# Relu² attention into a gated MLP on one core: 32 more score tiles of the first batch are read back transposed, VectorE rounds some high parts, the first phases are placed anew, and first pairs' own blocks are computed at 128 columns

## The chip, the cores and the metric

The kernel runs on one core of one Trainium2 chip. The metric is device time in microseconds (us). Before the change three runs gave a median of 2008.58 us (2007.91 to 2011.16). The profiled execution, from which all rows below come, took 2007.14 us, of which the traced span is 2005.4 us.

## The reference, cut to what matters

```
scores = (1/S) * z @ z.T                    # 4 batches, S = 3008, z has 64 columns
attn   = maximum(scores, 0) ** 2
x      = u * (attn @ v)                     # v, u: 256 columns
xn     = x / sqrt(mean(x*x) + 1e-6) * rms_g
out    = (silu(xn @ w_gate) * (xn @ w_val)) @ w_out     # 1536 hidden columns
```

The score matrix of a batch is z times its own transpose, so it is symmetric, and so is `attn`.

## The kernel before, in words

**Tiling.** The 3008 tokens of a batch are six query chunks of 512 (the last has 448), taken two at a time: a *pair* `p` is two chunks `k = 0, 1`, numbered `c0` and `c0 + 1`, and a batch has three pairs (`NP = 3`), twelve in all. The keys are 24 tiles `kt` of 128. Phase A of a pair runs 24 *steps*, one per key tile in the order that `order(p)` gives, and each step treats both chunks.

**One step.** For each chunk TensorE makes a 128x512 block of scores in PSUM by two matmuls (L537 with the high part of z, L538 with the low part). ScalarE takes the relu (L549). The square is either VectorE's product of relu and PSUM (L557), or, where the string `SQUARED` has a 1, two ScalarE squares (L580 and L588). Every operand of a later matmul is split into a rounded high part `H` and a low part `L`: ScalarE casts the high part (L582, or the square at L580 gives it), VectorE subtracts (L594). Then six matmuls accumulate attn times v (L674, L675 and L679, twice each). In program order a step `i` emits the scores of step `i + 2` (`emit_s`), the split of step `i + 1` (`emit_l`), the jobs hung on the step, and the value matmuls of step `i` (`emit_av`).

**Kept tiles.** A block computed for query chunk `c` and a key tile of a later chunk `kc` can serve, transposed, as the block of query chunk `kc` and the key tiles of chunk `c`. `keep_tile` makes a copy in 2-byte halves (VectorE L648 or ScalarE L650, as the string `COPIES` says), SyncE's queue stores it to HBM (L654, L656), and `load_turned` reads two key tiles at once by a transposing DMA (L492) into one of six `T` buffers; the block then needs no score matmuls, no relu and no square. In batches 1 to 3 all such blocks are kept; in batch 0 only those that the set `KEPT` lists. A chunk's *own* block (its queries against its own keys) is symmetric in itself: for all chunks but the first of a batch and those of pair 0, the last two of its four key tiles are computed at 256 columns only, and the other half comes transposed from the first two (`keep_half`, `load_half`).

**Phases.** The program runs phase A of pairs 0, 1 and 2 (batch 0) first, then alternates: phase M (the MLP) of pair 0, phase A of pair 3, M of pair 1, A of pair 4, and so on. Beside the first three phases A the kernel prepares the MLP's weights: they are loaded, decoded by five VectorE operations per piece (L216 to L235), added and combined by GpSimd or VectorE (`pool_pieces`, L179 and L183), cast by ScalarE (L297) and stored to HBM (L305). At which of the 72 steps of these phases each of these jobs, each load and each read-back is emitted is read in turn from the table `PLAN` by `place`. Each engine runs its instructions in program order, and SyncE's queue issues its DMAs in program order.

Of the kernel before, what the change touches and what calls it, by code (L numbers as in the profile page):

```python
# [19 lines left out]
P = 128  # L20
CH = 512
# [21 lines left out]
]  # L43
SQUARED = [
    ["000010001101001011110110", "011011110101111001111101"],
    ["010010111011111101100110", "011001011110010110100101"],
    ["100111011011001110101010", "111111110111111101010101"],
]
RESIDENT = [
    ["000000000100000011001000", "000100100000001101001001"],  # L50
    ["101010101000000101000010", "100001000011011010000101"],
    ["101000110101000101101010", "000010001101001000000010"],
]
KEPT = {(4, 5)}
# [11 lines left out]
def kernel(  # L66
# [80 lines left out]
    def hook(phase, slot):  # L147
        if phase[0] == "D":
# [308 lines left out]
    LEADS = (7, 1, 4, 5, 0), (7, 1, 3, 6, 0), (7, 1, 4, 5, 0)  # L457

    def order(p):
        b, c0 = where(p)[:2]  # L460
        if p == 0:
            return list(range(NK))
        first = list(range(4 * (c0 + 1), min(4 * (c0 + 2), NK)))
        last = list(range(4 * c0, 4 * c0 + 4))
        rest = [k for k in range(NK) if k not in first and k not in last]
        turns = [k for k in rest if k < 4 * c0]
        keeps_ = [k for k in rest if k >= 4 * c0]
        of = dict(F=first, L=last, T=turns, K=keeps_)
        return [of[x].pop(0) for x in PATTERNS[c0 // 2]]

    def is_half(p, i, k):

        c, kt = where(p)[1] + k, order(p)[i]
        return p > 0 and c > 0 and kt // 4 == c and kt % 4 >= 2
# [6 lines left out]
    def is_turned(p, i, k):  # L481
        b, c0 = where(p)[:2]
        kc = order(p)[i] // 4
        return kc < c0 + k and keeps(b, kc, c0 + k)

    def load_turned(p, i, k):
        b, c0 = where(p)[:2]
        kt, c = order(p)[i], c0 + k
# [17 lines left out]
    def is_square(p, i, k):  # L506

        return p < LAG and SQUARED[p][k][i] == "1" and not is_turned(p, i, k) and not is_half(p, i, k) and i < NK - 2

    def in_psum(p, i, k):  # L510

        b, c0 = where(p)[:2]
        if p >= LAG or RESIDENT[p][k][i] != "1":
            return False
        c, kt = c0 + k, order(p)[i]
# [8 lines left out]
    def s_product(p, i):  # L524
        b, c0 = where(p)[:2]
        kt = order(p)[i]
        for k in range(2):
            if is_turned(p, i, k):
# [6 lines left out]
            cols = slice(HALF if is_half(p, i, k) else 0, n)  # L535
# [32 lines left out]
    copies = [0]  # L568

    def emit_l(p, i, ks=(0, 1)):  # L570
        b, c0 = where(p)[:2]
        kt = order(p)[i]
        made_ = {}
        highs = {}
        for k in ks:
            n = width(c0 + k)
            a = made_[k] = att[p, i, k]
            hi = highs[k] = moving.tile([P, CH], F32R, tag="H", name="H", bufs=5)
            if is_square(p, i, k):
# [9 lines left out]
        for k in ks:  # L589
            n = width(c0 + k)  # L590
            a, hi = made_[k], highs[k]
            if kt < NK - 1:
# [7 lines left out]
        for k, a in made_.items():  # L600
            c = c0 + k
            n = width(c)
            kc = kt // 4
            if kc == c and c and p > 0 and kt % 4 < 2:
# [3 lines left out]
                def keep_half(a=a, c=c, m=n - HALF):  # L608
# [31 lines left out]
    def keep_tile(b, c, kt, c0, a):  # L640
# [3 lines left out]
        halves = copy_tile(LAG if b or c0 else 0, ("out", "out", "out", "u"))  # L644
# [8 lines left out]
        if b == 0:  # L653
# [753 lines left out]
```

## Time and profile before

| what | value |
|---|---|
| median of three runs | 2008.58 us |
| the profiled execution | 2007.14 us, its span 2005.4 us |
| phases A of pairs 0, 1, 2 | 5.06 to 94, to 180, to 256.95 us |
| phase M of pair 0; phase A of pair 3 | to 346.76; to 431.03 us |
| TensorE busy | 1998.6 us, 8976 matmuls |
| VectorE, ScalarE busy | 1595.5, 1417.0 us |
| GpSimd busy | 166.2 us |
| DMA | 328.37 MB in 355822 packets |

The page gives busy time per engine; the stages above are cut where TensorE's first score matmul of a phase A, or the first MLP matmul of a phase M, starts. Matmuls overlap in the trace, so the time that one takes is read from the starts of successive matmuls and not from its recorded duration. The same holds in part for VectorE and ScalarE, whose successive instructions overlap by about 0.1 us.

### The profile page before, as it was taken

To read this page: it belongs to the slowest core of one execution; us is meant where nothing else is said; L and a number is where in the kernel's file an instruction comes from. 1 tells how busy PE (TensorE), PEld (TensorE's weight loads), DVE (VectorE), ACT (ScalarE), POOL (GpSimd) and SP (SyncE) were. 2 spreads that over 40 slices of the span, in tenths; PEclk is the share of its full clock that TensorE was granted. 3 is DMA by queue.
4 is the path that set the end of the run, shared out by engine and by line. 5 is a ranking of instruction groups with operands and counts; after the bars stand their busy time and mean duration, and the time that the engine had idled before them with its cause. 6 is when DMAs were issued, how large, how long until landed. Compare 5 with 4: busy or idle time off the path is not lost.

```text
span 2005.4 us, 27191 instructions
## 1 busy us (share of the span) xinstructions
PE 1998.6 (100%) x8976; PEld 1672.8 (83%) x8976; DVE 1595.5 (80%) x2712; ACT 1417.0 (71%) x2593; POOL 166.2 (8%) x308
## 2 busy tenths in 40 slices
PE   9999999999999999999999999999999999999999
PEld 7888888888888888888888888888888888888889
DVE  8899888988867877887886786788778687677776
ACT  8898877875766666697575665779658566567565
POOL 0254306000000002100000000310000000000000
PEclk9999999999999999999999999999999999999999
DMA  4245574473484696247347469624644846844343
GB/s 155 78 136 165 132 254 135 150 240 120 122 220 155 162 217 233 90 147 232 136 126 200 168 151 242 211 98 153 225 133 125 214 153 162 205 152 153 123 162 115
DMA packets 355822, 328.37 MB, mean 164 GB/s; under 512 B 222944, under 2 KB 272480, under 8 KB 355680
## 3 DMA queue, kind: packets, MB, share of 16 engines
q1 hardware_dynamic: 355680, 326.64, 54.0%
q8 instruction: 70, 1.15, 0.2%
q14 instruction: 72, 0.59, 0.1%
HBM read 189.73 MB, written 85.72 MB: 137 GB/s over the span
## 4 chain that ended last, share of the span: by engine, by line
PE 99%; ACT 1%; DVE 0%; DMA 0%; issue 0%; SPq 0%; ACTq 0%; DVEq 0%
PE po L674 13%; PE po L675 13%; PE po L679 12%; PE ps L904 11%; PE ps L905 11%; PE ps L906 11%; PE py L932 6%; PE py L933 6%; PE py L936 6%; PE ps L538 4%; PE ps L537 4%; DMA raw<-in_zT 0%; ACT r L549 0%; ACT H L580 0%; PE ps L784 0%
## 5 line engine op out<-in xcount | busy, mean ns | idle before, releaser
L674 PE MATMUL po<-H,vh 128*128 128x512 f32 (+1 forms) x1152 | 446.2, 387 | 0.8 <-ACT H L580 0.8
L675 PE MATMUL po<-H,vl 128*128 128x512 f32 (+1 forms) x1152 | 445.5, 387 | 0.0
L911 ACT COPY s<-ps 128x512 f32<-128x512 f32 (+1 forms) x432 | 249.7, 578 | 208.6 <-PE ps L906 208.3
L904 PE MATMUL ps<-xh,wu 128*128 128x512 f32 (+1 forms) x1008 | 389.7, 387 | 0.0
L905 PE MATMUL ps<-xh,wu 128*128 128x512 f32 (+1 forms) x1008 | 388.4, 385 | 0.0
L906 PE MATMUL ps<-xl,wu 128*128 128x512 f32 (+1 forms) x1008 | 388.3, 385 | 0.0
L679 PE MATMUL po<-L,vh 128*128 128x512 f32 (+1 forms) x1104 | 336.0, 386 | 0.1
L916 ACT CAST hH<-s 128x512 fp32r<-128x512 f32 (+1 forms) x288 | 176.6, 613 | 195.9 <-DVE s L1001 187.6
L921 DVE TENSOR_TENSOR hL<-s,hH 128x512 fp32r<-128x512 f32 (+1 forms) x288 | 198.9, 691 | 96.7 <-ACT hH L916 85.3
L549 ACT ACTIVATE r<-ps 128x512 f32<-128x512 f32 x354 | 195.7, 594 | 97.7 <-PE ps L538 81.2
L674 PEld LDWEIGHTS po<-H,vh 128*128 128x128 f32 x1152 | 216.4, 188 | 43.1 <-ACT H L580 1.6
L675 PEld LDWEIGHTS po<-H,vl 128*128 128x128 f32 x1152 | 216.8, 188 | 39.8
L679 PEld LDWEIGHTS po<-L,vh 128*128 128x128 f32 x1104 | 207.2, 188 | 40.2 <-DVE L L594 1.0
L557 DVE TENSOR_TENSOR r<-ps,r 128x512 f32<-128x512 f32 (+1 forms) x265 | 173.8, 683 | 71.0 <-ACT r L549 70.3
L932 PE MATMUL py<-hH,woh 128*128 128x512 f32 (+1 forms) x576 | 222.1, 386 | 0.3 <-ACT hH L916 0.3
L933 PE MATMUL py<-hH,wol 128*128 128x512 f32 (+1 forms) x576 | 221.8, 385 | 0.0
L904 PEld LDWEIGHTS ps<-xh,wu 128*128 128x128 f32 x1008 | 189.3, 188 | 37.7 <-ACT s L911 2.2
L906 PEld LDWEIGHTS ps<-xl,wu 128*128 128x128 f32 x1008 | 189.3, 188 | 36.1
L905 PEld LDWEIGHTS ps<-xh,wu 128*128 128x128 f32 x1008 | 189.4, 188 | 36.0 <-DMA wu<-wc 0.7
L594 DVE TENSOR_TENSOR L<-r,H 128x512 fp32r<-128x512 f32 (+1 forms) x301 | 200.1, 693 | 9.7 <-ACT r L588 9.4
L936 PE MATMUL py<-hL,woh 128*128 128x512 f32 (+1 forms) x576 | 174.9, 385 | 0.0
L995 DVE TENSOR_TENSOR s<-s 128x512 f32<-128x512 f32 (+1 forms) x144 | 98.0, 680 | 80.3 <-ACT s L911 79.9
(107 smaller groups left out, 2935.0 us busy)
## 6 DMA issues: line engine op xcount, KB each, us to landing
wu<-wc SPq DMA_DIRECT2D x288, 448.0 KB, 4.0
kept<-halves SPq DMA_DIRECT2D x168, 256.0 KB, 2.1
raw<-in_v SPq DMA_DIRECT2D x44, 256.0 KB, 4.1
out_T<-y SPq DMA_DIRECT2D x44, 256.0 KB, 2.0
raw<-in_zT SPq DMA_DIRECT2D x38, 256.0 KB, 4.3
u<-in_uT SPq DMA_DIRECT2D x36, 256.0 KB, 4.0
ux<-xg SPq DMA_DIRECT2D x14, 512.0 KB, 4.2
wc<-wohi SPq DMA_DIRECT2D x21, 256.0 KB, 2.9
```

The lines of the kernel that those rows point to most:

```text
L594: nc.vector.tensor_tensor(lo[:, :n], a[:, :n], f32(hi[:, :n]), op=ALU.subtract)
L674: nc.tensor.matmul(po[d][:, :n], wh[:, j, ds], hi[:, :n], start=(i == 0), stop=False)
L675: nc.tensor.matmul(po[d][:, :n], wl[:, j, ds], hi[:, :n], start=False, stop=(ends and lo is None))
L679: nc.tensor.matmul(po[d][:, :n], wh[:, j, ds], lo[:, :n], start=False, stop=ends)
L904: nc.tensor.matmul(ps[:, :n], wh[:, o, :], xh[:, :n], start=start, stop=False, skip_group_check=True)
L905: nc.tensor.matmul(ps[:, :n], wl[:, o, :], xh[:, :n], start=False, stop=False, skip_group_check=True)
L906: nc.tensor.matmul(ps[:, :n], wh[:, o, :], xl[:, :n], start=False, stop=stop, skip_group_check=True)
L911: nc.scalar.copy(s, ps[:, :self.n])
L921: nc.vector.tensor_tensor(lo[:, :self.n], s, f32(self.h[h][0][:, :self.n]), op=ALU.subtract)
L932: nc.tensor.matmul(acc[h, d][:, :n], woh[f // 4][:, f % 4, ds], hi[:, :n], start=(f == 0), stop=False)
L933: nc.tensor.matmul(acc[h, d][:, :n], wol[f // 4][:, f % 4, ds], hi[:, :n], start=False, stop=False)
L936: nc.tensor.matmul(acc[h, d][:, :n], woh[f // 4][:, f % 4, ds], lo[:, :n], start=False, stop=(f == NF - 1))
```

## The change

1. `KEPT` grows from one pair of chunks to nine: eight more blocks of four key tiles in batch 0. The 32 tiles are computed once in phases A of pairs 0 (12) and 1 (20), copied, stored, and read back transposed in pair 1 (8) and pair 2 (24): 12 of 448 columns, 20 of 512.
2. `SQUARED` may now hold 2 or 3: VectorE casts the high part (L627) in place of ScalarE, 2 after a ScalarE square, 3 after a VectorE product. 17 tiles do so.
3. `PLAN`, `SQUARED`, `RESIDENT`, `MAGNITUDES`, `ADDERS`, `COPIES`, `HALVES` and `QUERIES` hold other values: jobs of the first three phases stand at other steps, and some move between ScalarE, VectorE and GpSimd.
4. In the first pair of batches 1 to 3 (pairs 3, 6 and 9) both chunks' own blocks are computed from 128, 256 and 384 columns on (`first_column`), and what is left out is read back transposed. The two chunks of such a pair go through the key tiles in different orders (`FINE`). Stores of kept tiles in those pairs are issued a step later (`late`).

```diff
-KEPT = {(4, 5)}
+KEPT = {(1, 3), (1, 4), (1, 5), (2, 3), (2, 4), (2, 5), (3, 4), (3, 5), (4, 5)}
...
 SQUARED = [
-    ["000010001101001011110110", "011011110101111001111101"],
+    ["003102122001121211002010", "022121010200111311111201"],
...
+    FINE = "XXXXKOKKKKKOKKKKKOKKKKKO", "KOKKKKKOKKKKKOKKKKKOXXXX"
+    def is_fine(p):
+        return p >= LAG and p % NP == 0
...
+    def first_column(p, i, k):
+        c, kt = where(p)[1] + k, order(p, k)[i]
+        if kt // 4 != c or p == 0:
+            return 0
+        if not is_fine(p):
+            return HALF if c and kt % 4 >= 2 else 0
+        return kt % 4 * P
...
     def load_half(p, i, k):
+        if is_fine(p):
+            r = order(p, k)[i] % 4
+            t = work.tile([P, 2, 2 * CH], U16, tag="T", name="T", bufs=6)[:, 0, :]
+            nc.sync.dma_start_transpose(
+                out=t[:, :2 * r * P], in_=diagonal[b, c0 + k][:2 * r * P, r * P:(r + 1) * P]
+            )
...
-            cols = slice(HALF if is_half(p, i, k) else 0, n)
+            cols = slice(first_column(p, i, k), n)
...
+            if is_copied(p, i, k):
+                nc.vector.tensor_copy(hi[:, :n], a[:, :n])
...
-        if b == 0:
+        if b == 0 or c0 == 0:
             late.append(lambda rows=rows, part=halves[:m]: nc.sync.dma_start(out=rows, in_=part))
...
+                if is_turned(p, i, k) and i % 2 == 0:
+                    at(ph, i - 7, lambda p=p, i=i, k=k: load_turned(p, i, k))
+                elif is_half(p, i, k):
+                    at(ph, i - 5, lambda p=p, i=i, k=k: load_half(p, i, k))
```

What the tables do to the order shows at three places. TensorE, last own tile of the first chunk in pair 3 (`zst` is the z of its keys, `po` the value sums), before:

```order
L537 MATMUL ps<-mh,zst_3238 128x512
L538 MATMUL ps<-ml,zst_3238 128x512
L674 MATMUL po<-H,vh_3552 128x512
L675 MATMUL po<-H,vl_3613 128x512
L674 MATMUL po<-H,vh_3552 128x512
L675 MATMUL po<-H,vl_3613 128x512
L679 MATMUL po<-L,vh_3552 128x512 x2
```

and of the change:

```order
L569 MATMUL ps<-mh,zst_3182 128x128
L570 MATMUL ps<-ml,zst_3182 128x128
L726 MATMUL po<-H,vh_3998 128x512
L727 MATMUL po<-H,vl_4000 128x512
L726 MATMUL po<-H,vh_3998 128x512
L727 MATMUL po<-H,vl_4000 128x512
L731 MATMUL po<-L,vh_3998 128x512 x2
```

The two score matmuls have 128 columns in place of 512; the value matmuls beside them are of another key tile, as wide as before.

VectorE in the first steps of pair 1, after the two pairs of gate products that end pair 0 (`wt`, `wraw`, `w`, `wolo` belong to the MLP's weights, `halves` are copies of kept tiles, or of own tiles at 2x256), before:

```order
L557 TENSOR_TENSOR ps<-ps,r 128x512
L218 TENSOR_SCALAR wt<-wt 128x512
L219 TENSOR_SCALAR wt<-wt 128x512
L594 TENSOR_TENSOR L<-r,H 128x512 x2
L179 TENSOR_TENSOR w_462<-w_794,w_462 128x512
L615 COPY halves<-r 128x2x256
L557 TENSOR_TENSOR r<-ps,r 128x512 x2
L594 TENSOR_TENSOR L<-ps,H 128x512
L594 TENSOR_TENSOR L<-r,H 128x512
```

and of the change, beginning a few rows behind the gate products:

```order
L218 TENSOR_SCALAR wt<-wt 128x512
L219 TENSOR_SCALAR wt<-wt 128x512
L225 SCALAR_TENSOR_TENSOR wraw<-wraw,wt 128x512
L231 TENSOR_SCALAR wt<-wraw 128x512
L235 SCALAR_TENSOR_TENSOR wraw<-wraw,wt 128x512
L630 TENSOR_TENSOR L<-r,H 128x512 x2
L700 COPY halves<-r 128x1024 x2
L179 TENSOR_TENSOR wolo<-w_775,wohi 128x512
L179 TENSOR_TENSOR w_1259<-wraw 128x512
L179 TENSOR_TENSOR w_1261<-wraw 128x512
L667 COPY halves<-r 128x2x256
L630 TENSOR_TENSOR L<-r,H 128x512 x2
```

The products of the square are gone from this stretch (ScalarE squares), and decoding, weight sums and copies of kept tiles stand between the `L` that TensorE needs. From the program step of TensorE's value matmuls 25 to 29 (of 72), VectorE has 30 instructions of two sources or of 1024 halves, 9 of one source (`TENSOR_SCALAR`) and 2 of 2x256 halves, where it had 23, 4 and 1; ScalarE has 10 relus, 29 casts and squares and 2 copies of kept tiles.

SyncE's queue in the middle of pair 1, where before no tile was read back from the kept ones (`wc` are stores of weights, `u` loads for the gates), of the change:

```order
L706 DMA kept_1624<-halves 128x1024
L512 DMA_TRANSPOSE T<-kept_1140 128x2x1024 x2
L706 DMA kept_1621<-halves 128x1024
L706 DMA kept_1624<-halves 128x1024
L512 DMA_TRANSPOSE T<-kept_647 128x2x1024
L753 DMA u<-in_uT 128x512
L706 DMA kept_1621<-halves 128x1024
L706 DMA kept_1624<-halves 128x1024
L512 DMA_TRANSPOSE T<-kept_647 128x2x1024
```

Stores of tiles that pair 2 will read and transposing loads for pair 1 stand one behind the other. In the three phases there are now 18 transposing loads of kept tiles (2 before) and 36 stores (4 before).

## Rows read from the trace of the kernel before

**Rows 1.** The page's first part: TensorE's busy time, share, count

```profile
PE 1998.6 (100%) x8976; PEld 1672.8 (83%) x8976; DVE 1595.5 (80%) x2712; ACT 1417.0 (71%) x2593; POOL 166.2 (8%) x308
```

**Rows 2.** The page's chain that ended last, by engine

```profile
PE 99%; ACT 1%; DVE 0%; DMA 0%; issue 0%; SPq 0%; ACTq 0%; DVEq 0%
```

**Rows 3.** Stages: length, busy PE, PEld, DVE, ACT, POOL (instructions), clock, DMA share, GB/s

```profile
5.06:94.00 88.94, 88.47 (x385) 72.02 (x385) 77.48 (x128) 76.53 (x146) 14.51 (x28) 1.00 0.35 111
94.00:180.00 86.00, 85.95 (x383) 70.79 (x382) 80.26 (x142) 75.23 (x146) 38.30 (x65) 1.00 0.48 140
180.00:256.95 76.95, 76.11 (x352) 65.10 (x351) 67.59 (x113) 70.16 (x141) 29.38 (x52) 1.00 0.59 166
...
346.76:431.03 84.27, 84.27 (x375) 69.75 (x374) 79.91 (x143) 75.03 (x127) 4.41 (x8) 1.00 0.50 168
...
687.69:754.11 66.42, 66.42 (x309) 57.28 (x308) 50.21 (x88) 44.76 (x84) 0.00 (x0) 1.00 0.93 220
```

**Rows 4.** TensorE in order of time (start us, us, instruction): 512 columns

```profile
480.34 0.39 PE L904 MATMUL ps<-xh,wu 128*128 128x512 f32 x1
480.57 0.39 PE L905 MATMUL ps<-xh,wu 128*128 128x512 f32 x1
480.80 0.39 PE L906 MATMUL ps<-xl,wu 128*128 128x512 f32 x1
481.02 0.39 PE L932 MATMUL py<-hH,woh 128*128 128x512 f32 x1
```

**Rows 5.** The same view: score matmuls of 448 columns

```profile
210.44 0.37 PE L537 MATMUL ps<-mh,zst 128*128 128x448 f32 x1
210.64 0.36 PE L538 MATMUL ps<-ml,zst 128*128 128x448 f32 x1
210.84 0.40 PE L674 MATMUL po<-H,vh 128*128 128x512 f32 x1
```

**Rows 6.** The same view: matmuls of 256, 192 and 384 columns

```profile
117.70 0.28 PE L537 MATMUL ps<-mov,zst 128*128 128x256 f32 x1
117.82 0.28 PE L538 MATMUL ps<-mov,zst 128*128 128x256 f32 x1
117.94 0.40 PE L674 MATMUL po<-H,vh 128*128 128x512 f32 x1
...
203.85 0.25 PE L537 MATMUL ps<-mh,zst 128*128 128x192 f32 x1
203.94 0.28 PE L538 MATMUL ps<-ml,zst 128*128 128x192 f32 x1
204.05 0.42 PE L674 MATMUL po<-H,vh 128*128 128x512 f32 x1
...
1949.91 0.33 PE L906 MATMUL ps<-xl,wu 128*128 128x384 f32 x1
1950.08 0.34 PE L932 MATMUL py<-hH,woh 128*128 128x384 f32 x1
```

**Rows 7.** VectorE and ScalarE in order of time: instructions back to back

```profile
87.61 1.28 DVE L594 TENSOR_TENSOR L<-r,H 128x512 fp32r<-128x512 f32 x2
86.75 2.18 ACT L582 CAST H<-r 128x512 fp32r<-128x512 f32 x4
```

**Rows 8.** Groups by line and shape, 0 to 560 us: busy us, mean ns

```profile
L650 ACT COPY halves<-r 128x1024 uint16<-128x1024 uint16 x29 | 30.3, 1056 | 0.0
L648 DVE COPY halves<-r 128x1024 uint16<-128x1024 uint16 x20 | 13.7, 686 | 0.0
L218 DVE TENSOR_SCALAR wt<-wt 128x512 f32<-128x512 f32 x18 | 8.3, 461 | 0.3
L380 DVE TENSOR_SCALAR mh<-raw 128x512 fp32r<-128x512 f32 x6 | 2.7, 456 | 2.5 <-DMA raw<-in_zT 2.5
```

**Rows 9.** TensorE in order of time, with the idle time before it

```profile
184.67 0.44 PE L674 MATMUL po<-H,vh 128*128 128x448 f32 x1 [0.75 <-ACT H L580]
```

**Rows 10.** DMA queues and issues: share of 16 engines; median us to landing

```profile
q1 hardware_dynamic: 355680, 326.64, 54.0%
...
T<-kept SPq DMA_TRANSPOSE x92, 4.9
```

More of the change, by code (lines that the diff above doesn't have):

```diff
@@ L457, with order, make_order @@
     LEADS = (7, 1, 4, 5, 0), (7, 1, 3, 6, 0), (7, 1, 4, 5, 0)
-    def order(p):
+    FINE = "XXXXKOKKKKKOKKKKKOKKKKKO", "KOKKKKKOKKKKKOKKKKKOXXXX"
+    orders = {}
+    def is_fine(p):
+        return p >= LAG and p % NP == 0
+    def order(p, k):
+        if (p, k) not in orders:
+            orders[p, k] = list(make_order(p, k))
+        return orders[p, k]
+    def make_order(p, k):
         b, c0 = where(p)[:2]
         if p == 0:
[L462 to L469, printed above, removed]
+            return range(NK)
+        own = list(range(4 * c0, min(4 * (c0 + 1), NK)))
+        other = list(range(4 * (c0 + 1), min(4 * (c0 + 2), NK)))
+        turns, keeps_ = list(range(4 * c0)), list(range(4 * (c0 + 2), NK))
+        if not is_fine(p):
+            of, pattern = dict(F=other, L=own, T=turns, K=keeps_), PATTERNS[c0 // 2]
+        else:
+            if k:
+                own, other = other, own
+            of, pattern = dict(O=own, X=other, K=keeps_), FINE[k]
+        return [of[x].pop(0) for x in pattern]
+    def first_column(p, i, k):
+        c, kt = where(p)[1] + k, order(p, k)[i]
+        if kt // 4 != c or p == 0:
+            return 0
+        if not is_fine(p):
+            return HALF if c and kt % 4 >= 2 else 0
+        return kt % 4 * P
     def is_half(p, i, k):
-        c, kt = where(p)[1] + k, order(p)[i]
-        return p > 0 and c > 0 and kt // 4 == c and kt % 4 >= 2
+        return first_column(p, i, k) > 0
     HALF = CH // 2
@@ L482, in is_turned @@
         b, c0 = where(p)[:2]
-        kc = order(p)[i] // 4
+        kc = order(p, k)[i] // 4
         return kc < c0 + k and keeps(b, kc, c0 + k)
@@ L487, in load_turned @@
         b, c0 = where(p)[:2]
-        kt, c = order(p)[i], c0 + k
+        kt, c = order(p, k)[i], c0 + k
         n = width(c)
@@ L506, in is_square, with is_copied @@
     def is_square(p, i, k):
-        return p < LAG and SQUARED[p][k][i] == "1" and not is_turned(p, i, k) and not is_half(p, i, k) and i < NK - 2
+        return p < LAG and SQUARED[p][k][i] in "12" and not is_turned(p, i, k) and not is_half(p, i, k) and i < NK - 2
+    def is_copied(p, i, k):
+        return p < LAG and SQUARED[p][k][i] in "23"
     def in_psum(p, i, k):
         b, c0 = where(p)[:2]
-        if p >= LAG or RESIDENT[p][k][i] != "1":
+        if p >= LAG or RESIDENT[p][k][i] != "1" or is_copied(p, i, k):
             return False
-        c, kt = c0 + k, order(p)[i]
+        c, kt = c0 + k, order(p, k)[i]
         if is_turned(p, i, k) or is_half(p, i, k) or kt == NK - 1:
@@ L525, in s_product @@
         b, c0 = where(p)[:2]
-        kt = order(p)[i]
         for k in range(2):
+            kt = order(p, k)[i]
             if is_turned(p, i, k):
@@ L568 @@
     copies = [0]
+    LATE = 15
     def emit_l(p, i, ks=(0, 1)):
         b, c0 = where(p)[:2]
-        kt = order(p)[i]
         made_ = {}
@@ L591, in emit_l @@
             a, hi = made_[k], highs[k]
-            if kt < NK - 1:
+            if is_copied(p, i, k):
+                nc.vector.tensor_copy(hi[:, :n], a[:, :n])
+            if order(p, k)[i] < NK - 1:
                 lo = moving.tile([P, CH], F32R, tag="L", name="L", bufs=5)
@@ L602, in emit_l, with keep_own, keep_half @@
             n = width(c)
+            kt = order(p, k)[i]
             kc = kt // 4
-            if kc == c and c and p > 0 and kt % 4 < 2:
+            if kc == c and is_fine(p) and kt % 4 < 3:
+                if (b, c) not in diagonal:
+                    diagonal[b, c] = dram.tile([6 * P, CH], U16, tag=f"own{c}", name=f"own{c}")
+                def keep_own(a=a, c=c, n=n, r=kt % 4):
+                    q = (r + 1) * P
+                    halves = copy_tile(p, ("ws", "wt"))
+                    nc.vector.tensor_copy(
+                        halves[:, :, q:n], a[:, q:n].bitcast(U16).rearrange("p (q h) -> p h q", h=2)
+                    )
+                    rows = diagonal[b, c][2 * r * P:2 * (r + 1) * P, :].rearrange("(p h) q -> p h q", h=2)
+                    late.append(lambda: nc.sync.dma_start(out=rows[:, :, q:n], in_=halves[:, :, q:n]) and None)
+                at(("A", p), max(i - 1, 0), keep_own)
+            elif kc == c and c and p > 0 and kt % 4 < 2:
                 if (b, c) not in diagonal:
                     diagonal[b, c] = dram.tile([CH, HALF], U16, tag=f"diag{c}", name=f"diag{c}")
-                def keep_half(a=a, c=c, m=n - HALF):
+                def keep_half(a=a, c=c, kt=kt, m=n - HALF):
                     halves = copy_tile(p, ("ws", "wt"))
@@ L662, in emit_av @@
         n = width(c0 + k)
-        kt = order(p)[i]
+        kt = order(p, k)[i]
         if i == 0:
@@ L1140 @@
         j = c0 // 2
-        for i in range(0, NK, 2):
+        for i in range(0, NK, 2) if not is_fine(p) else ():
             for k in range(2):
@@ L1150 @@
                     else:
-                        own = order(p)[i] // 4 == where(p)[1]
+                        own = order(p, k)[i] // 4 == where(p)[1]
                         after = PATTERNS[j].rindex("F") + LEADS[j][1] if own else 0
```

39 lines of the change are left out of this document (22 added, 17 removed), and 26 rows, old and new, of the table PLAN.

## Prediction

> **What bounds the kernel now.** I read the page's engine table first: TensorE is busy for 1998.6 of 2005.4 us [rows 1], and the chain that ended last is TensorE for 99% [rows 2]. Busy time of overlapping matmuls alone would not prove a bound, so I then read successive starts: three matmuls of 512 columns take 0.68 us, 0.227 us each, with no hole [rows 4]. The stages [rows 3] say the same: the column after the length is TensorE's busy time, and it fills each stage but for 0.5, 0.05 and 0.8 us in the first three. What idles there is small; the largest single hole in pairs 0 to 2 is 0.75 us where pair 2 begins, ended by a ScalarE square [rows 9]. So the time is the sum of the matmuls, and a matmul taken away is worth its spacing as long as the other engines keep up. In pairs 0 and 1 VectorE is busy for 87% and 93% of the stage, ScalarE for 86% and 87% [rows 3]: there the cover is thin.
>
> **The 32 tiles.** Each drops two score matmuls. 20 tiles have 512 columns: 40 x 0.227 = 9.1 us. 12 have 448; their spacing is 0.20 us (0.40 from the first start to the third [rows 5]): 24 x 0.20 = 4.8 us. Together 13.9 us, in pairs 1 and 2.
>
> **Own blocks in pairs 3, 6 and 9.** A pair of score matmuls at 512 columns takes 0.454 us [rows 4], at 384 columns 0.34, at 256 columns 0.24, at 192 columns 0.20 (start to the start of the matmul behind the pair) [rows 6]. No row has 128 columns: above, it is bounded by the 0.20 of 192 columns, below by 0.12, half of 256. From 256 to 192 columns the pair fell by 0.04, so I take 0.17, near the upper end. The first chunk goes from 512, 512, 512, 512 to 512, 384, 256, 128: 0.11 + 0.21 + 0.28 = 0.60 us. The second goes from 512, 512, 256, 256 to the same: 0.11 + 0.07 = 0.18. Three pairs: 3 x 0.78 = 2.3 us (2.2 to 2.5). The row shows a 192-column matmul followed 0.09 us later by one with the same key block [rows 6]. The Trainium skill, "TensorE: Matmul & The Clock Gate", section "LDWEIGHTS (loading the stationary operand)", says that a load of 128 columns of weights takes about 128 / 1.2 = 107 ns; if every narrow matmul had to wait for such a load, a 128-column pair would take 0.21 us and this term would be 2.1 us. By that rule two matmuls could not be 0.09 us apart, and the trace has them so; I keep 2.3.
>
> **What VectorE, ScalarE and the queues pay.** Prices: two VectorE subtractions back to back take 1.28 us, 0.60 each beyond the first's lead-in; four ScalarE casts 2.18, 0.52 each [rows 7]; a copy into halves has 0.69 on VectorE (0.60 back to back, like the subtraction of nearly the same duration) and 1.06 on ScalarE (0.95) [rows 8]. A cast by VectorE (L627) is not in the trace. It has one source, as the scaling L380 at 0.46 [rows 8]; below that I set 0.23, half of it, above 0.60, the two-source price; I take 0.43, being nearest in shape. Over pairs 0 to 2 VectorE loses 24 products (-14.3 us) and gains 17 casts (+7.3) and 24 copies (+14.1); with a handful of weight jobs exchanged with ScalarE and GpSimd it ends about 5 us up. ScalarE loses 32 relus, 16 casts or squares to `H`, 8 second squares, and gains 8 copies and 5 magnitudes: about 15 us down. Averaged over the three phases that fits: VectorE 225.3 us of busy time (the first three stages of [rows 3] summed) plus 5, against 251.9 - 13.9 = 238 us. GpSimd does not grow.
>
> It does not fit everywhere. At program steps 25 to 29, the first of pair 1, I counted the change's order: VectorE has 30 x 0.60 + 9 x 0.42 + 2 x 0.35 = 22.5 us (9 one-source operations as L218, 0.46 less some overlap [rows 8]), ScalarE 10 x 0.49 + 29 x 0.52 + 2 x 0.95 = 21.9, TensorE 80 x 0.227 = 18.2. Before, VectorE had 23 x 0.60 + 4 x 0.42 + 0.35 = 15.8 there. So VectorE falls 4.3 us behind, ScalarE 3.7 at the same time. A lead absorbs part: in a plain step VectorE needs 4 x 0.60 = 2.4 of TensorE's 3.6 us, and TensorE's first four value matmuls of a chunk (0.9 us) do not need `L`: 2.1 us. **The stall is 4.3 - 2.1 = 2.2 us.** Queued behind the late `L` are the next steps' products, and behind those TensorE's scores, since PSUM has four score buffers. The steps behind (30 to 32, 8.2 us of VectorE for 10.5 of TensorE) refill the lead; steps 33 to 36 ask for 1.4 us too much of ScalarE, which the lead covers. Over all of pairs 0 and 1, though, the same count adds 11.5 us to VectorE's 157.7, that is 169 of 171 us (174.9 less 8 x 0.454). In pair 3 VectorE runs at 79.91 of 84.27, 95%, with no TensorE idle [rows 3]. If 95% were all that these steps can hold, pairs 0 and 1 would need 178 us, 6.8 us more. Busy time shrinks when instructions follow closely (0.60 in place of 0.68), so I do not take all of it: **I take 4 us of stall in all**, between 0 (the lead and closer packing absorb everything) and 9 (6.8 + 2.2).
>
> The DMA side I cost at nothing, with this cover: 16 more transposing loads and 20 more stores fall in pairs 1 and 2 (12 stores in pair 0, whose share is 0.35 [rows 3]). At the average of 326.64 MB in 54.0% of the span [rows 10] a megabyte takes 3.3 us of all queues, a 0.26 MB store 0.87. In pair 5's stage 220 GB/s x 66.42 us = 14.6 MB take 61.8 us [rows 3]; 9.9 MB of it are 18 loads of 0.52 MB and two small ones, and taking 3.3 for the rest leaves 2.45 us a load. Pairs 1 and 2 have 0.48 x 86 + 0.59 x 77 = 86.7 us of DMA work and get 20 x 0.87 + 16 x 2.45 = 56.6: 143 of 149 us (162.95 less 13.9), 96%, little over pair 5's 93%, at which TensorE never idled. A load lands 4.9 us after its issue [rows 10]; in SyncE's order the first of pair 1 stands two steps (some 7 us) before ScalarE reads it. The new wait in pairs 3, 6 and 9, a relu that writes into the buffer its transposed part lands in, has three steps for a store and a load; behind it in ScalarE's queue stand the casts of the step before.
>
> **The sum.** 2007.14 (profiled execution) - 13.9 - 2.3 + 4.0 = 1994.9 us. The median of the runs shown lies 1.4 us above that execution, so 1996.3 us.
>
> **The rivals.** *No stall:* VectorE's work is early work for the most part (weights), the lead is larger than I count, and all 16.2 us come through: 1992.4. For it: pair 3 at 95%. Against: five steps with both helpers 20% over TensorE. *VectorE becomes the bound in pairs 0 and 1:* the 6.8 us of the 95% limit and the 2.2 us of the early steps add up: 2007.14 - 16.2 + 9 + 1.4 = 2001.4. For it: 169 of 171 us; against: ScalarE is relieved by 15 us, and part of VectorE's waits for ScalarE goes with that. *The transposing loads end later than TensorE (other side):* in pairs 1 and 2 DMA work is 143 of 149 us. It decides from 2.45 + (5.7 + 16.2) / 16 = 3.8 us a load on: there it has eaten the gain. At the 4.9 us that a load needs alone [rows 10], if nothing ran beside it, work is 182, 33 us over, and the time about 2025. Against: pair 5 has 18 such loads in 66 us [rows 3], which at 4.9 would be 88. A milder form (3.0 us a load) costs 3 us and leaves 1999.
>
> **How the numbers follow.** This kernel's measurement can tell about 0.2%, 4 us, from no change. My case, 1993.5 to 1999.5: 0.52. No stall: 0.20. VectorE's bound: 0.17, of which 0.02 lie beyond 2004.6. DMA: 0.11, of which 0.05 slower than before, 0.05 within 0.2%, 0.01 faster. Slower I hold at 0.05, the same at 0.08, faster at 0.87. The range reaches below to the full sum with a microsecond for the holes that pair 2's start has today, 1991.3, above to the second rival with some more: 2003. Outside are about 0.14, most of it above.
>
> **What would show it.** Right: score matmuls in pairs 0 to 2 down by 64, a 128-column pair at 0.16 to 0.20 us, the stages of pairs 3, 6 and 9 shorter by 0.8 us, holes in TensorE of some microseconds in all between 94 and 130 us, ended by ScalarE's `H` or VectorE's `L`. Wrong: no hole there (the lead was larger), holes all over pairs 0 and 1 with VectorE near 100% (second rival), or holes ended by a `T` load or by a copy waiting for its buffer, with a DMA share near 1 from 130 us on (third). The forecast also fails if narrow matmuls are as slow as 512 columns; that would take back only 2.3 us.

## The result and the profile after

The changed kernel takes 2019.48 us (median of 4 runs, 2016.88 to 2020.26), the kernel before 2008.76 beside it: ratio 1.0051 (95% interval 1.004 to 1.0063). It is 10.7 us slower where 12.3 us less than the 2008.58 of before were forecast. From the page of the kernel after: engines, the DMA queue, the chain that ended last, and two groups of matmuls (busy, mean ns, idle before them).

```profile
PE 1994.2 (99%) x8912; PEld 1660.5 (82%) x8912; DVE 1603.3 (79%) x2734; ACT 1399.1 (69%) x2551; POOL 173.6 (9%) x308
q1 hardware_dynamic: 401728, 345.78, 57.7%
PE 88%; DMA 4%; DVE 3%; ACT 2%; issue 2%; POOL 1%; SPq 0%; DVEq 0%; ACTq 0%; POOLq 0%
L956 PE MATMUL ps<-xh,wu 128*128 128x512 f32 (+1 forms) x1008 | 390.4, 387 | 3.3 <-DMA wu<-wc 2.3
L731 PE MATMUL po<-L,vh 128*128 128x512 f32 (+1 forms) x1104 | 337.6, 387 | 6.8 <-DVE L L630 6.8
```

The 64 matmuls are gone, as in [rows 1] against this. But the chain is TensorE for 88% and no longer 99% [rows 2]: transfers, VectorE and ScalarE have entered it. By stages (columns as in [rows 3]; pair 1 begins near 95 us, pair 2 near 190, the first MLP stage at 262.19, pair 3 at 356.48):

```profile
5.07:95.00 89.93, 89.65 (x384) 73.13 (x384) 80.48 (x137) 75.49 (x140) 9.34 (x17) 1.00 0.41 141
95.00:145.00 50.00, 43.77 (x186) 33.42 (x185) 46.86 (x79) 45.84 (x85) 17.49 (x28) 1.00 0.62 191
145.00:190.00 45.00, 42.77 (x181) 34.18 (x180) 41.07 (x77) 34.19 (x65) 21.06 (x35) 0.96 1.05 240
190.00:262.19 72.19, 67.61 (x308) 56.14 (x306) 64.89 (x103) 51.54 (x101) 35.37 (x54) 1.00 0.90 227
262.19:356.48 94.29, 92.11 (x396) 75.27 (x397) 73.07 (x114) 64.42 (x117) 36.67 (x72) 0.98 0.59 197
356.48:440.08 83.60, 83.60 (x376) 69.42 (x374) 79.93 (x146) 73.23 (x126) 4.42 (x8) 1.00 0.51 168
```

Pairs 0 to 2 end at 262.19 where they ended at 256.95 [rows 3]: 5.2 us later, not 13.9 earlier. Two stretches stand out. From 95 to 145 us VectorE is busy for 46.9 and ScalarE for 45.8 of 50 us and TensorE idles for 6.2. From 145 to 190 us the transfers fill all 16 engines (a share of 1.05 by the profile's count), from there to 262.19 us 0.90 of them, and TensorE idles for 2.2 and 4.6 us more. The waits of TensorE in two windows, 95 to 155 and 262 to 300 us (us in total, times, longest):

```profile
PE po L731 <- DVE L L630: 5.2, 6, 1.7
PE po L726 <- ACT H L614: 0.6, 1, 0.6
...
PE ps L956 <- DMA wu<-wc: 2.3, 1, 2.3
PE ps L957 <- DMA wu<-wc: 2.2, 2, 1.5
```

The first two are late helpers; the others are the MLP's first weights, late at the start of a stage that had no such wait before. Between them, in order of time, a hole near the end of pair 1, and the row of stages for the stretch behind it:

```profile
175.23 1.24 SPq L530 DMA_TRANSPOSE T<-diag  x1
...
178.40 0.38 ACT L581 ACTIVATE T<-ps 128x256 f32<-128x256 f32 x1 [2.75 <-DMA T<-diag]
...
179.36 0.50 PE L726 MATMUL po<-H,vh 128*128 128x512 f32 x1 [1.42 <-ACT H L614]
...
182.54 0.63 PE L727 MATMUL po<-H,vl 128*128 128x512 f32 x1
182.97 0.63 PE L726 MATMUL po<-H,vh 128*128 128x512 f32 x1
183.40 0.63 PE L727 MATMUL po<-H,vl 128*128 128x512 f32 x1
...
181.10:184.50 3.40, 3.40 (x8) 2.72 (x9) 3.30 (x9) 1.69 (x4) 0.00 (x0) 0.50 1.23 263
```

A load of pair 1's own block is issued at 175.23, ScalarE stands for it for 2.75 us, and all that is queued behind (the casts to `H`) is late with it: TensorE waits 1.42 us. After that hole, and a second of 0.53, matmuls start 0.43 us apart instead of 0.227 until 184.6: half clock, 1.2 GHz (0.50 in the last row), 1.3 us more. The load is late because its store was. SyncE's queue stood at such loads for their stores' landing, in the kernel after from 95 to 275 us (first row), in the kernel before from 95 to 260 us (second):

```profile
SPq L530 <- DMA diag<-halves: 8.4, 5, 4.2
...
SPq L502 <- DMA diag<-halves: 12.0, 4, 4.6
```

It stood there even longer before, and TensorE waited for none of it. But there was little to spare: pair 1's load was issued at 163.99, landed some 3 us later, and ScalarE needed it at 167.54. Its store had landed 3.4 us after its issue; after the change the two stores take 4.8 and 5.1 us, and the margin of half a us is gone.

**A budget.** For each trace I summed, over all successive matmul starts, what exceeds the spacings of [rows 4 to 6]. Before it is 14.0 us in all, after 42.2. That 28.2 us more, less the 13.9 and about 1.9 us of work saved, is 12.4: the spans differ by 12.1 (2005.4, 2017.5). Each row is one execution. How far executions differ is seen in e2 and e15 (below), which leave the first three phases as the changed kernel has them: there the same sum gives 10.3 and 10.0 us from 60 to 150 us, 9.9 and 9.3 to 250, 5.5 and 5.2 to 300. In us:

| kernel | to 60 us | 60–150 | 150–250 | 250–300 | behind | all |
|---|---|---|---|---|---|---|
| before | 3.7 | 0.5 | 2.7 | 0.2 | 6.9 | 14.0 |
| after | 4.9 | 9.3 | 8.6 | 7.8 | 11.6 | 42.2 |
| e3 plain loads | 4.0 | 10.2 | 3.5 | 4.2 | 16.4 | 38.3 |
| e4 no decode | 3.8 | 10.1 | 9.8 | 4.3 | 11.6 | 39.6 |
| e12 no preparation | 3.4 | 4.2 | 10.0 | 5.5 | 11.7 | 34.9 |
| e13 both, weights earlier | 3.5 | 4.2 | 4.8 | 0.1 | 12.4 | 24.9 |
| e14 own blocks, earlier | 4.1 | 0.6 | 2.8 | 0.1 | 8.0 | 15.6 |

### The profile page after: what moved, and what is told of

It is laid out like the page before. It is cut to its first block, busy times and chain, and to the rows that moved or that the text cites. A ratio compares the mean times of both kernels' runs of the same rounds, so it can differ in the third digit from the quotient of the medians.

```text
span 2017.5 us, 27153 instructions
## 1 busy us (share of the span) xinstructions
PE 1994.2 (99%) x8912; PEld 1660.5 (82%) x8912; DVE 1603.3 (79%) x2734; ACT 1399.1 (69%) x2551; POOL 173.6 (9%) x308
## 2 busy tenths in 40 slices
DMA packets 401869, 347.50 MB, mean 172 GB/s; under 512 B 263552, under 2 KB 314624, under 8 KB 401728
## 4 chain that ended last, share of the span: by engine, by line
PE 88%; DMA 4%; DVE 3%; ACT 2%; issue 2%; POOL 1%; SPq 0%; DVEq 0%; ACTq 0%; POOLq 0%
PE ps L956 11%; PE ps L957 11%; PE ps L958 11%; PE po L726 10%; PE po L727 10%; PE po L731 10%; PE py L984 6%; PE py L988 6%; PE py L985 6%; PE ps L570 3%; PE ps L569 3%; DMA wu<-wc 1%; DVE L L630 1%; DMA u<-in_uT 1%; DMA diag<-halves 1%
## 5 line engine op out<-in xcount | busy, mean ns | idle before, releaser
L963 ACT COPY s<-ps 128x512 f32<-128x512 f32 (+1 forms) x432 | 249.8, 578 | 214.6 <-PE ps L958 214.0
L731 PEld LDWEIGHTS po<-L,vh 128*128 128x128 f32 x1104 | 206.7, 188 | 50.6 <-DVE L L630 11.6
L581 ACT ACTIVATE r<-ps 128x512 f32<-128x512 f32 (+1 forms) x310 | 173.1, 597 | 89.0 <-PE ps L570 84.2
L589 DVE TENSOR_TENSOR r<-ps,r 128x512 f32<-128x512 f32 (+1 forms) x231 | 151.5, 682 | 66.1 <-ACT r L581 65.9
L630 DVE TENSOR_TENSOR L<-T,H 128x512 fp32r<-128x512 f32 (+1 forms) x262 | 170.6, 682 | 28.9 <-ACT H L616 27.0
L630 DVE TENSOR_TENSOR L<-r,H 128x512 fp32r<-128x512 f32 x268 | 177.2, 688 | 4.4 <-ACT r L622 2.2
```

Of the source, the lines that this page charges most:

```text
L630: nc.vector.tensor_tensor(lo[:, :n], a[:, :n], f32(hi[:, :n]), op=ALU.subtract)
L731: nc.tensor.matmul(po[d][:, :n], wh[:, j, ds], lo[:, :n], start=False, stop=ends)
L963: nc.scalar.copy(s, ps[:, :self.n])
```

## Experiments

Medians stand with the ratio to the kernel before on the same chip; the changed kernel's is 1.0051.

**The parts apart.** e1: all tables of the kernel before, `FINE` kept. e2: `is_fine` returns `False`, all else as changed.

> Part of the change alone: the kept set, the plan of early jobs and all the engine tables are those of the kernel before; the first pairs of batches 2 to 4 get their own blocks at 128-column steps. In the changed kernel the stages of pairs 3, 6 and 9 are 0.67, 0.62 and 0.61 us shorter, but from the start of pair 3's stage to the last matmul it needs 1657.3 us where the kernel before needed 1655.0. Theory 'the gain is given back where it is made' (the loads that the new order moves make the MLP stages behind it wait): the same here, 2.3 us slower than before, about 2011. Rival 'the predicted term holds, the loss there came from the tables': 1.9 to 2.3 us faster, about 2006.7.

> The other part alone: kept tiles, high parts by VectorE and the new plan as in the changed kernel; the first pairs of batches 2 to 4 keep the own blocks of the kernel before. Theory 'given back where it is made': 2.3 us faster than the changed kernel, about 2017.2, pairs 0 to 2 as long as in it (257.1 us, and 94.3 us for the first MLP stage). Rival 'the tables did all the harm': about 2021.5, 2 us over the changed kernel.

e1 took 2008.64 us, 0.9999 (0.999 to 1.0008); e2 2018.56, 1.0049 (1.0035 to 1.0062). The tables, with the kept tiles, do the harm; the own blocks bring nothing that can be measured. Neither expectation for them held: 2.3 us lost lie outside e1's interval, 1.9 us won at its edge.

**Transfers.** e3 loads as many bytes in 1 KB rows (896 bytes in the last chunk), without transposing:

```
+        if p < LAG:
+            rows = kept[b, c, kt // 4][:2 * n, :].rearrange("(r h) q -> r h q", h=2)[:, 1, :]
+            for j, lo in enumerate((0, n - 256)):
+                nc.sync.dma_start(out=t[:, j, :2 * n]..., in_=rows[lo:lo + 256, :n]...)
```

> The changed kernel, but in pairs 1 and 2 the loads of kept tiles are plain loads of the same number of bytes into the same buffers, in the same order, and don't transpose (the tiles' numbers are then not those of the reference). Engine work is untouched. Theory 'two causes': the holes ended by transfers go (3.9 us where pair 2 begins, 2.3 us at 200 to 210 us, 5 us at the start of the first MLP stage and 1.7 behind it), the eight holes of 7.5 us ended by VectorE or ScalarE in pair 1 stay: 2007 to 2011. Rival 'VectorE alone' (transfers are late because everything is): 2018 to 2020. Rival 'transfers alone' (VectorE is late because its copies wait for buffers that stores hold): all holes go, 1998 to 2000.

2012.0 us, 1.0017 (1.0008 to 1.0025): 7.5 us won, 1 us short of what two causes asked for and far from both rivals. The holes of pair 1 stay; those from 150 to 300 us shrink from 16.4 to 7.7 (table; the profiled execution, the longest of eleven at 2015.74 us, has 4.8 us more of late starts behind 300 us than the changed kernel's). Stages of e3:

```profile
95.00:145.00 50.00, 43.21 (x182) 32.74 (x181) 45.97 (x77) 45.07 (x84) 16.57 (x25) 1.00 0.60 185
145.00:190.00 45.00, 44.69 (x198) 36.09 (x197) 43.37 (x81) 37.76 (x73) 23.51 (x38) 1.00 0.87 267
190.00:255.84 65.84, 63.08 (x291) 53.08 (x290) 61.50 (x99) 48.23 (x95) 34.01 (x51) 1.00 0.75 230
```

The share falls from 1.05 to 0.87 and from 0.90 to 0.75, and TensorE's idle time from 2.2 to 0.3 us in the second row. The edit relieves SyncE's queue too. What it took to issue these loads from 95 to 265 us (ns min/median/max), changed kernel and e3:

```profile
L512 SPq DMA_TRANSPOSE T<-kept x18: 1468/2050/4598, 148.5 to 240.9; - x18
...
L515 SPq DMA_DIRECT2D T<-kept x36: 517/602/1079, 148.7 to 235.0; - x36
```

A transposing load holds the queue for 2.05 us in the median, the two plain ones in its place for 1.2 together, and whatever stands behind is issued that much later. No run separates the engines' load from this.

**VectorE.** e4:

```
 def fields():
+    nc.vector.tensor_scalar(wl, wl, 0x3FFFFFFF, None, op0=ALU.bitwise_and)
-    ... (two operations)
+def join(): pass
+exponent = lower = join
```

> The changed kernel, but the decoding of the MLP weights on VectorE is left out: five operations of 2.5 us a piece are replaced by one of 0.43 us, in all 16 pieces (the weights are then not those of the reference). That takes some 10 us of VectorE's work out of pair 1 and as much out of pair 0; transfers are untouched. Theory 'two causes': the 7.5 us of holes in pair 1 ended by VectorE go, those ended by transfers stay: 2010 to 2013. Rival 'VectorE alone': all of it goes, 1998 to 2000. Rival 'transfers alone': 2017 to 2020.

2016.58 us, 1.0038 (1.0025 to 1.005). Only 2.9 us, with an interval that overlaps the changed kernel's, though VectorE's work in pairs 0 to 2 fell from 233.3 to 196.3 us. Two causes as I had put them would have given more, VectorE alone far more; by the time 'transfers alone' (2017) is nearest. Pair 1's holes stayed for the most part: of the 10.1 us in the table some 2.6 are matmuls at half clock (third row), so the holes are 7.5 us for 9.3. Of e4: a row of its stages and one of VectorE's waits in it, the row at half clock, and TensorE's two longest waits from 95 to 155 us:

```profile
94.00:121.00 27.00, 24.89 (x106) 19.14 (x104) 19.24 (x33) 23.73 (x45) 7.33 (x14) 1.00 0.57 173
...
DVE L L615 <- ACT r L607: 3.0, 1, 3.0
...
124.20:131.00 6.80, 6.23 (x16) 4.89 (x16) 5.20 (x10) 5.11 (x11) 0.00 (x0) 0.50 0.53 186
...
PE po L711 <- ACT H L599: 2.5, 2, 2.0
PE po L716 <- DVE L L615: 1.7, 3, 0.6
```

VectorE has 7.8 us to spare and now stands for ScalarE's second squares, and TensorE's longest wait there is for ScalarE's `H` (in the changed kernel 0.6 us, with 5.2 for VectorE's `L`). So VectorE was not the limit alone. e5 adds to e4 `SQUARED[1][1] = "000000000011111101000101"`:

> As e4_no_decode (decoding of the MLP weights on VectorE left out), and in pair 1 nine squares of the second chunk's first 12 tiles go from ScalarE (cast-square and second square) to VectorE (product), which has room there now: ScalarE loses 0.52 us and VectorE gains 0.60 us a tile. In e4 the holes of pair 1 stayed, with ScalarE busy for 23.7 of the 27 us behind 94 us, and VectorE waiting for ScalarE's second squares (up to 3.0 us). Theory 'both helpers are full there, each limits when the other is relieved': the holes before 115 us (0.6, 0.6, 0.7, 0.8 us) go, those ended by transfers stay: 2012 to 2014. Rival 'the holes of pair 1 come from the queue of transfers': as e4, 2016 to 2017.

2015.33 us, 1.0033 (1.0021 to 1.0046): between the two expectations, and no more than 1.3 us under e4, with overlapping intervals. The holes before 115 us are 2.8 us in sum in both. e6 is e5 with e3's loads:

> e5_balanced and e3_plain_loads together: relieved helpers in pair 1, and the kept tiles of pairs 1 and 2 loaded plainly instead of transposing (the tiles' numbers are not those of the reference). Theory 'helpers and transfers, two causes that add up': e3 took 7.5 us off, e4 2.9, balance some 3 more: 2004 to 2007. Rival 'one hides the other': the time falls by more than the sum, to the forecast without stalls, 1993 to 1998. Rival 'a third cause': above 2010.

2006.58 us, 0.9995 (0.9987 to 1.0004): 8.75 us under e5, as the plain loads gave 7.5 alone. The two add up.

**Copies on GpSimd.** `if b == 0 and c0 == 2:` the two halves by `nc.gpsimd.tensor_copy`; e11 is e6 with that and e7's edit.

> The changed kernel, with the 16 copies of kept tiles of pair 1 on GpSimd (busy for 7 of the 26 us behind 95 us there) and not on VectorE or ScalarE: some 11 us of their work in pair 1 go, transfers stay. Theory 'both helpers are full in pair 1': its holes of 7.5 us shrink to 3 or less, 2014 to 2016. Rival 'GpSimd's copies slow VectorE (0.69 to 0.89 us an operation where both work, in the changed kernel's trace) and come late': 2018 to 2022.

> All reliefs together: e6_all (weights not decoded, squares balanced in pair 1, kept tiles loaded without transposing; the numbers are not the reference's), the weights of the first MLP stage one step earlier, and pair 1's kept copies on GpSimd. Theory 'helpers and transfers account for all of it': 2006.6 less 2.2 (what the earlier weights won in the changed kernel) less 3 to 5 of pair 1's remaining holes: 1999 to 2002. Rival 'a third cause': 2005 or more.

2024.41 us, 1.0079 (1.0066 to 1.0091), and 2013.3, 1.0024 (1.0014 to 1.0035): the rival of e10 was right in kind, and the loss is larger than it said. Its trace has 40 half copies on GpSimd, so 20 copies moved, not 16. e11, with the same move in it, was no closing sum at all. GpSimd is no help for VectorE here: the same subtraction from 95 to 150 us (busy us, mean ns), changed kernel and e10:

```profile
L630 DVE TENSOR_TENSOR L<-r,H 128x512 fp32r<-128x512 f32 x21 | 14.5, 724 | 0.7 <-ACT H L616 0.4 <-ACT r L622 0.3
...
L630 DVE TENSOR_TENSOR L<-r,H 128x512 fp32r<-128x512 f32 x19 | 16.4, 897 | 0.4 <-ACT H L616 0.4
```

**The early work of all helpers.** e12 replaces decoding, sums, casts and differences of the second and third weight group by nothing; loads and stores stay:

```
-            g = place(g + (was == "A"), op[3], kind)
+            g = place(g + (was == "A"), skip if left_out else op[3], kind)
-            g = place(max(...), high)
+            g = place(max(...), skip if j else high)
```

> The changed kernel without the preparation of the second and third group of MLP weights on VectorE, ScalarE and GpSimd (their raw loads stay, and stores of the same bytes in the same places, from another tile; the MLP's numbers are not the reference's). e4 and e5 took only VectorE's part of it, and ScalarE's magnitudes and casts, up to 4.5 us between two steps, stayed. Theory 'the pile-up of early work on both helpers makes pair 1's holes, without the lead that the forecast counted on': the holes there (8.7 us from 95 to 150 us) shrink to 2 us or less, those ended by transfers stay: 2009 to 2012. Rival 'pair 1's holes come from the kept tiles' own copies and transfers': they stay, 2015 or more.

2011.33 us, 1.0013 (1.0005 to 1.0022), as expected; pair 1's holes fall by half, from 9.3 to 4.2, not to 2. GpSimd is relieved with the two others, so e12 does not tell its part. Stages of e12:

```profile
95.00:145.00 50.00, 47.68 (x207) 37.54 (x206) 37.80 (x61) 47.78 (x90) 7.63 (x12) 1.00 0.72 220
145.00:190.00 45.00, 43.82 (x194) 35.47 (x193) 28.46 (x56) 28.93 (x56) 0.00 (x0) 1.00 1.04 240
```

ScalarE is still at 47.8 of 50 in the first row (kept copies, relus and squares of a pair that now gets more done): that this makes the other 4.2 us is argued, not shown. In the second VectorE and ScalarE are idle for a third and TensorE still idles for 1.2 us, with the transfers at 1.04. e13 is e12 with e3's loads and e7's edit:

> e12_no_prep, with plain loads for the transposing ones of pairs 1 and 2 (e3) and the first MLP stage's weights one step earlier (e7). Theory 'pile-up and late transfers together are all': 2019.5 less 7.5 to 9 (pile-up), 7.5 (e3) and 2.2 (e7): 2000 to 2003, with pairs 0 to 2 within 4 us of the 238.0 us that the forecast's matmul terms leave. Rival 'a third cause': 2006 or more.

2000.53 us, 0.9962 (0.9949 to 0.9974), as expected. Pairs 0 to 2 take 241.75 us (5.06 to 246.81), 3.8 over the 238.0 of the matmul terms. What is left there has no tested cause, and neither have the 5.5 us of late starts that e13 has more than the kernel before behind 300 us (table).

**The first MLP weights.** e7: `NK - (4 if c0 == 0 or p < LAG else 3) + f`.

> The changed kernel, with the four loads of MLP weights that the first MLP stage starts with issued one program step (3.6 us) earlier. Theory 'a backlog of transfers makes them late': the hole at the start of the stage (2.5, 0.9 and 0.4 us, and 1.4 us at half clock behind it) shrinks by 3.6 us or goes: 2015 to 2016. Rival 'they wait for their buffers': SyncE stops at them for as long, nothing is won, and the loads behind come later: 2018 to 2021.

2017.3 us, 1.0038 (1.0025 to 1.005): 2.2 us less, between the two expectations, and the interval overlaps the changed kernel's. In its trace the first MLP stage is 91.8 us long (94.3): the stage gained, the whole not clearly.

**The own blocks' gain.** e9: e1 with `if b == 0:` for the late stores and `NK - 3 + f`. e14: e1 with `NK - (5 if f == 0 and c0 == 0 else 4 if c0 == 0 else 3) + f`.

> As e1_own_only (own blocks alone, the rest of the kernel before), but two lines that came with them are set back: the stores of kept tiles in pairs 3, 6 and 9 are issued at once and not at the next step, and the first MLP weights of the stage behind them one step later, as before. In e1 each of the three stages is 0.6 to 0.7 us shorter, and the whole is not: MLP and attention stages elsewhere are 0.2 to 0.9 us longer. Theory 'the two lines cost what the own blocks save': 1.9 us faster than before, about 2006.7. Rival 'the loss lies elsewhere (small waits for MLP weights that differ from run to run)': as e1, 2008 to 2009. Rival 'the lines were needed': the weights come late, 2010 or more.

> As e1_own_only, with the very first MLP weights behind pairs 3, 6 and 9 issued one more step earlier, ahead of a store of a kept tile for which SyncE stands 3.3 us. e9 showed that a step later costs 5 us in each of these stages. Theory 'the own blocks save 1.9 us, given back where weights come just too late': 2006.5 to 2007.5. Rival 'the weights' buffers aren't free then': SyncE stops at them, the loads of own tiles come late, 2008.6 to 2012.

e9 took 2023.49 us, 1.0079 (1.0065 to 1.0093): its last expectation, and worse. TensorE's waits over the whole of e9:

```profile
PE ps L956 <- DMA wu<-wc: 8.8, 3, 2.9
PE ps L957 <- DMA wu<-wc: 2.0, 4, 0.6
```

Three waits of up to 2.9 us, one at each MLP stage behind the fine pairs, and half clock after each: 24.9 us of late starts behind 360 us. A fine pair and its MLP stage together are 4.9 to 5.5 us longer than in e1. The first of these weights are issued at 430.07 us (425.66 in e1), about a step later. But e9 sets back both lines: that the place of these loads alone is worth 5 us a stage is argued. e14 took 2007.84, 0.9998 (0.9989 to 1.0007): its trace has the three MLP stages at 90.0 to 90.1 us, as before (e1 had up to 90.9) and a span of 2004.7, but the median says no more than "not slower".

**A smaller dose.** e8: `is_fine` returns `False`, all tables of the kernel before, `KEPT = {(3, 4), (3, 5), (4, 5)}`, the new loads five steps ahead of their use. What the change does to SyncE's order for pairs 3, 6 and 9 stays in it: the later stores, and the first MLP weights a step earlier. e15 and e16 set back `copies[0] % 5`, by 32 in the changed kernel and by 8 in e8.

> A smaller dose: the kernel before, with its plan and tables, keeps two more blocks, those of chunk 3 with chunks 4 and 5 (8 tiles: 8 copies and stores in pair 1, 4 transposing loads in pair 2, 16 score matmuls less, 8 x 0.227 + 8 x 0.20 = 3.4 us). Theory 'a kept tile is worth its two matmuls while helpers and transfers have room': 2005 to 2006. Rival 'each kept tile costs more than it saves': 2009 to 2012.

> e8_two_blocks with the same running count set back by its 8 more copies. In e8 pairs 0 to 2 are 2.1 us longer and the stages from pair 3 on 3.1 us (pair 5 alone 2.0). Theory 'the shifted choice': the latter go, about 2010; what stays is what two more blocks cost in pairs 0 to 2. Rival: 2013 as e8.

> The changed kernel with one expression altered that the change touches without naming it: in batches 2 to 4 a running count of copies, modulo 5, decides whether VectorE or ScalarE copies a kept tile, and the count now starts 32 higher, so that other copies fall to VectorE than before. Here the 32 are taken off again. From pair 3 to the last MLP stage the changed kernel needs 1403.6 us, the one before 1401.3, with the own blocks' 1.9 us saved. Theory 'the shifted choice makes the later stages wait': 2 to 3 us faster than the changed kernel, 2016.5 to 2017.5, pairs 5 and 8 at 66.4 us again (66.8 and 67.2 in it). Rival 'their MLP weights are late for other reasons': no change, 2018.5 to 2020.

e8 took 2013.3 us, 1.0025 (1.0016 to 1.0035), e16 2014.82, 1.0034 (1.0021 to 1.0048), e15 2016.61, 1.0043 (1.003 to 1.0057). My theory of the shifted choice falls: e16 is not faster than e8. e15's median does lie where the theory put it, but its interval overlaps the changed kernel's, its stages from pair 3 on take 1403.3 us (1403.6 without the edit), and pairs 5 and 8 take 67.0 and 66.7, not 66.4. So 8 kept tiles, whose matmuls are 3.4 us, already cost more than they save. In e8's trace pairs 0 to 2 get 2.1 us longer; in e16's, with the same order of instructions up to there, 5.2. Pair 5 needs 68.4 and 68.7 us for 66.4 in a batch whose kept blocks the edit doesn't touch. Why pair 5 does is open; SyncE's order that stays in e8 is not tested apart.

## Why the prediction was wrong

**Right.** 64 matmuls fewer. Also the sums of work: VectorE in pairs 0 and 1 takes 80.48 + 46.86 + 41.07 = 168.4 us (169 forecast). Transfers in pairs 1 and 2 take 0.62 x 50 + 1.05 x 45 + 0.90 x 72.19 = 143.2 us of all engines (143 forecast, at 2.45 us a transposing load).

**Wrong, "I take 4 us of stall in all".** From 60 to 150 us late starts grew by 8.8 us. Forecast was a lag of 4.3 us at steps 25 to 29 and a lead of 2.1 against it. There was no lead: pair 1 begins with a hole (99.13 us, 0.65), and from there to 118.6 us the holes are 5.3 us, the whole lag and a little. (That first hole stays in e12: TensorE waits there for VectorE's gate products, not for the weights' work.) From 95 to 115 us VectorE is busy for 18.9 and ScalarE for 19.3 of 20 us:

```profile
95.00:115.00 20.00, 17.35 (x72) 12.61 (x71) 18.93 (x34) 19.30 (x36) 3.70 (x8) 1.00 0.44 142
```

e4 and e12 show what I had put into two separate sums to be one thing: both helpers are full in the same steps, and relieving one hands the limit to the other; relieving both, and GpSimd with them, gave 5.1 us.

**Wrong, "The DMA side I cost at nothing".** This step carries the most: 5.9 us more of late starts from 150 to 250 us, 7.6 from 250 to 300. My cover was an average, 143 of 149 us. The work is not spread so: the share is 0.62 up to 145 us and 1.05 in the next 45 us, since all 18 transposing loads come between 148 and 243 us. A store lands late there, the load of an own block waits for it in SyncE's queue, and ScalarE for that. What is late last are the first MLP weights, which [rows 10] does not name and the forecast did not look at. The four loads from 190 to 262 us with their median from issue to landing, kernel after (first row) and before (second):

```profile
wu<-wc SPq DMA_DIRECT2D x4, 448.0 KB, 7.6
...
wu<-wc SPq DMA_DIRECT2D x4, 448.0 KB, 5.1
```

They are issued from 255.46 us on, the first lands 6.7 us later, and TensorE, ready 2.3 us sooner, stands for it until 262.19. Before, the first was issued at 249.8, landed 4.1 us later and was used at 256.95. So two things went wrong: landing takes 2.6 us longer, and from issue to need there are 4.4 us where there were 7.2. e3 took 7.5 us off; e7's 2.2 are not clear of noise. The 7.6 us are at the upper end: with the same first phases e2 and e15 have 5.5 and 5.2 us of late starts from 250 to 300 us, where the kernel before has 0.2.

**The rivals** were priced as alternatives. "VectorE becomes the bound" (9 us of stall) came near in size (8.8), not in its mechanism: without the decoding VectorE had time to spare, and 7.5 us of holes stayed (e4). A backlog of transfers came too, though not by its rule (3.8 us a load): the sum of work is the one at 2.45. The two use different resources and add up, as e3, e12 and e13 show. The chance of 0.05 for slower allowed neither for their sum nor for loads that come late while the share over both pairs is below 1.

**Own blocks, -2.3.** The stages are shorter by 0.67, 0.62 and 0.61 us, 1.9 in all, not 2.3. A 128-column pair in the kernel after:

```profile
424.20 0.22 PE L569 MATMUL ps<-mh,zst 128*128 128x128 f32 x1
424.26 0.28 PE L570 MATMUL ps<-ml,zst 128*128 128x128 f32 x1
424.37 0.45 PE L726 MATMUL po<-H,vh 128*128 128x512 f32 x1
424.65 0.39 PE L727 MATMUL po<-H,vl 128*128 128x512 f32 x1
```

It takes 0.17 us to the next start, as forecast, and that matmul then takes 0.28 instead of 0.227: 0.22 in all, so 0.68 a stage by the same count. The rule that the forecast set against its row (the Trainium skill, "TensorE: Matmul & The Clock Gate", section "LDWEIGHTS (loading the stationary operand)": 107 ns a load, from which the forecast estimated 0.21 a pair) comes out nearer: the trace agrees in the total and in the 0.11 behind the second matmul, not in the 0.06 between the two. The forecast's argument against it misread the trace: it looked at the starts of the matmuls only. The weight loads around the 192-column pair of [rows 6], in the kernel before:

```profile
203.86 0.19 PEld L538 LDWEIGHTS ps<-ml,zst 128*128 128x128 f32 x1
203.97 0.19 PEld L674 LDWEIGHTS po<-H,vh 128*128 128x128 f32 x1
204.08 0.19 PEld L675 LDWEIGHTS po<-H,vl 128*128 128x128 f32 x1
```

They start 0.11 us apart, while the pair's matmuls stand 0.09 apart.

Behind 300 us late starts grew by 4.7 us all the same. That is not the own blocks' doing alone: by the same sum e1's trace has 2.6 us more there than the kernel before, and e2's, without them, 2.3. In e1's trace the 1.9 us saved are given back, and its median shows no gain. e9 shows that late MLP weights can do that, not that they do it in e1.

## What to carry to other kernels

Where a kernel is bound by one engine for 99%, ask of each helper and of the transfers not for the sum over a stage but for the worst few steps, and for the lead at the place where they begin; here a phase's first steps had none. Two rivals that use different resources are not alternatives: add their prices before giving a chance to the other side. A change of order can also take away lead: list the loads that the next stage starts with, and compare the time from issue to need with the time to landing under the new load.

## What the runs showed of the hardware

**VectorE beside GpSimd.** In the kernel after, 200 to 262 us, with GpSimd busy for half the time, the same subtraction (busy us, mean ns):

```profile
L630 DVE TENSOR_TENSOR L<-T,H 128x512 fp32r<-128x512 f32 x14 | 11.6, 831 | 1.0 <-ACT H L616 0.9
...
L630 DVE TENSOR_TENSOR L<-ps,H 128x512 fp32r<-128x512 f32 x4 | 2.8, 689 | 0.5 <-ACT ps L622 0.5
```

It takes 831 ns where it reads `T`, and 689 where it reads PSUM. From 400 to 560 us, where GpSimd has no work, the first takes 684 (13 operations). So beside GpSimd a kept tile's subtraction costs more than that of a tile whose product stayed in PSUM. The Trainium skill, "SBUF — State Buffer", section "SBUF: two separate sides", has the rule: a VectorE operation with two SBUF inputs and a GpSimd operation that reads SBUF lock each other out. The trace agrees: the subtraction with two SBUF inputs is slowed, the one that reads PSUM is not.

**Transposing loads.** With e3, transfers in pairs 1 and 2 take 0.60 x 50 + 0.87 x 45 + 0.75 x 65.84 = 118.5 us instead of 143.2: 1.4 us less for each of the 18 loads of 0.52 MB, and SyncE's queue is held for 1.2 us a load instead of 2.05. The Trainium skill, "Advanced Engine Details and Errata", section "X-Bar Transpose (TRN2)", says that transposing transfers are as fast as regular ones. These are not as fast as plain loads of the same bytes, and for them the measurement decides. But e3 changes two things at once. Its page has 34816 packets under 512 bytes fewer (228736 for 263552), which is what the 18 loads come to in pieces of 256 bytes; the plain loads read rows of 896 to 1024. How much is the transposing and how much the short pieces no run shows.
